# Planned durations of a list scheduler taken anew from a trace, in an attention kernel followed by two feed-forward blocks

## The chip, the cores and the metric

The kernel runs on one core of one Trainium2 chip, in one launch. The metric is device time in microseconds (us). Five engines work side by side: TensorE (PE, with its weight loads PEld), VectorE (DVE), ScalarE (ACT), GpSimd (POOL) and SyncE (SP, which issues the transfers). Each takes its instructions strictly in the order in which they were written.

## The reference

```
scores = q @ k.T / sqrt(64)              # 4 batches, 8 heads, 576 x 64, float32
kth    = the 32nd largest score of each row
attn   = softmax of the scores >= kth, 0 elsewhere
x      = (attn @ v), heads side by side   # 2304 tokens x 512
h      = x @ w_in;  g = max(0.01*h, h);  x = g @ w_out        # 512 -> 2048 -> 512
h      = max(x @ w1, x @ w2, x @ w3);    out = h @ w_out2     # 512 -> 768 -> 512
```

The weights are float64. The outputs are float32.

## The kernel before

**Work.** Attention is cut into 72 steps, numbered here 0 to 71, 18 to a batch; so steps 18, 36 and 54 open a new batch. A step takes 128 query rows of two heads, or 64 rows of four. Its parts are: the score product on PE (L702, two halves, j = 0 and j = 1), a copy of each half out of PSUM by ACT (L707, into one of three buffers S), the search for the 32nd largest score on DVE (L722 MAX8 and L724 MATCH_REPLACE8, seven rounds for each half), the exponential on ACT (L772), the mask (L777 on DVE for one half; L781 on DVE and L784 on POOL for the other), a split of the result in two float16 halves (L786 on ACT, L788 on POOL), a transposing transfer, the product with v on PE (L816 to L818) and its scaling (L823 and L825 on DVE, L827 on ACT).

The tokens that come out are grouped in 10 units (u = 0 to 9) of 192, 128, six times 256, 192 and 256 tokens. Each unit runs through both feed-forward blocks, on PE three float16 matmuls (L859 to L861) for each product: h (`h<-xu,wi`), y (`acc<-f16t,wo`), the three products m of the second block (`h<-k,w`, with a maximum on DVE, L1000), and o (`acc<-f16t,w`). Of float64 weights, DVE makes float32 by shifts on their two halves (L484, L487, L490: 42 pieces, so 126 instructions), ACT and POOL scale and split them (L352 to L354).

**What sets the order.** `Plan` is a list scheduler that runs when the kernel is built. Each piece of work is handed to `op(engine, duration, function, ...)` with a planned duration, what it reads and writes, and a due time `pr` (a step is due 11.9 us after the one before, `TA`). `Plan.run` then plays the engines forward with these durations: on each engine, of the pieces that could start at the earliest time (within `eps`, 0.03 us), the one with the lowest due time goes next, and a buffer is taken when the plan says that it is free. The planned start times give the order in which the instructions are written. The durations are not otherwise used: on the chip each engine runs its stream in that order and waits where data is late.

Durations come from small formulas:

```
def mm(n):                    return (n / 2.4 + MMO) / 1000
def act(n, psum=False, aps=0): return (n * 0.833 + (70 if psum else 120) + 105 * aps) / 1000
def dve(n, fast=False):       return (n / (2 if fast else 1) / 0.96 + 69) / 1000
def pool(n):                  return (n * 2.13 + 110) / 1000
```

The line numbers below are those of the kernel before; in the changed kernel every number from L49 on is higher by 3 (L722 is L725 there).

Of the kernel before, what the change touches and what calls it, by code (L numbers as in the profile page):

```python
# [14 lines left out]
AF = mybir.ActivationFunctionType  # L15
# [3 lines left out]
B, H, S, D = 4, 8, 576, 64  # L19
# [23 lines left out]


EPS = 0.03
MMO = 3.0
PQ = 100.0
PA = 100.0
PB = 0.0  # L49
# [22 lines left out]
class Plan:  # L72
# [50 lines left out]
    def run(self):  # L123
# [10 lines left out]
        while len(order) < total:  # L134
# [45 lines left out]
                    slots[b.tag].sort()  # L180
            for m in n.succ:
                m.nd -= 1
                m.ready = max(m.ready, end + self.LAT.get((n.eng, m.eng), 0.2))
                if m.nd == 0:
                    pend[m.eng].append(m)
        order.sort()
# [33 lines left out]
def attention_moe_kernel(ctx, tc, qk, v, w_in, w_out, w123, w2o, outT):  # L220
# [242 lines left out]
    def prep_w(kind, c, parts, hi, lo, colnorm, n2c, s, bi, pr, tags, guard=((), (), []), gate=()):  # L463
# [8 lines left out]
        for i, saps in enumerate(parts):  # L472
            nf = sum(n for _, n in saps)
            f = buf(tags[1], [P, 768 if tags[1] == "raw" else 512], I32)
            o = 0
            for sap, n in saps:
                raw = buf(tags[0], [P, 768])
                op(SP, 0.55, lambda raw=raw, sap=sap, n=n: Y.dma_start(raw().bitcast(I64)[:, :n], sap),
                   w=[raw, (key, "ld")] + ([(f, "ld")] if tags[1] in ("raw", "k2") or tags[0] == "raw" else []),
                   r=list(gate) + zr + (zf + [("l1", hp, a) for hp in range(HP) for a in range(2)] * (kind == "z") + guard[2] * (tags[1] == "raw") if kind in "tz" else []), pr=PRW0 if (kind, c) == ("i", 0) else pr,  # L480
                   dma=dma(P * n * 8))
                w = lambda raw=raw, n=n: raw().bitcast(I32)[:, :2 * n].rearrange("p (n t) -> p n t", t=2)
                t = lambda f=f, n=n, o=o: f()[:, o:o + n]
                op(DVE, dve(n, True), lambda w=w, t=t: V.tensor_scalar(  # L484
                    t(), w()[:, :, 1], 3, 0x3FFFFFFF, op0=ALU.logical_shift_left, op1=ALU.bitwise_and),
                   r=[raw] + zr + zf, w=[(f, o)], pr=pr)
                op(DVE, dve(n), lambda w=w, t=t: V.scalar_tensor_tensor(  # L487
                    t(), w()[:, :, 0], 29, t(), op0=ALU.logical_shift_right, op1=ALU.bitwise_or),
                   r=[raw] + zr + zf, w=[(f, o)], pr=pr)
                op(DVE, dve(n), lambda w=w, t=t: V.scalar_tensor_tensor(  # L490
                    t(), w()[:, :, 1], -0x40000000, t(), op0=ALU.bitwise_and, op1=ALU.bitwise_or),
                   r=[raw] + zr + zf, w=[(f, o)], pr=pr)
                for q in range(0, n, 512):
                    m = min(n - q, 512)
                    sq.append(((f, o), lambda f=f, q=q + o, m=m: f()[:, q:q + m].bitcast(F32), m))
                o += n
            fs.append((f, [(f, x) for x in np.cumsum([0] + [n for _, n in saps[:-1]]).tolist()],
                       lambda f=f, n=nf: f()[:, :n].bitcast(F32), nf))
# [181 lines left out]
    def attention(i):  # L680
# [10 lines left out]
        for j in range(2):  # L691
# [10 lines left out]
                            T.matmul(p()[osl, h, o:o + w], q()[:, hh, st, :n], k()[:, hh, kc:kc + w],  # L702
                                     start=st == 0, stop=st == 1, skip_group_check=True)

            op(PE, (0.5 if full else 0.7) * (COLD if i < NCOLD else 1), qk_, r=[k] + [(q, x) for x in range(3)], w=[p], pr=pq)
            t = Sb[j]
            op(ACT, act(S, True), lambda t=t, p=p: A.activation(t().rearrange("p (a s) -> p a s", a=2),  # L707
                                                               p()[:, :, :288], AF.Copy), r=[p], w=[(Sp, j)], pr=pq)
# [2 lines left out]
        if md == "N":  # L711
# [3 lines left out]
            for g in range(7):  # L715
                for j in range(2):
                    r = g // 2
                    mc = lambda j=j, r=r: m()[:, j, 8 * r:8 * r + 8]
                    src = (lambda j=j: Sb[j]()) if g < 2 else (lambda j=j: wj(j))
                    rd = [(Sp, j)] if g < 2 else [(wp, j, 0)]  # L720
                    if g % 2 == 0:
                        op(DVE, dve(S) * 1.03, lambda mc=mc, src=src: V.max(mc(), src()), r=rd, w=[(m, j, 0, r)], pr=pd)  # L722
                    else:
                        op(DVE, dve(S) * 1.03 + 0.06, lambda mc=mc, src=src, j=j: V.match_replace(  # L724
                            out=wj(j), in_to_replace=mc(), in_values=src(), imm_value=NEG),  # L725
                           r=[(m, j, 0, r)] + rd, w=[(wp, j, 0)], pr=pd)
        else:
# [73 lines left out]
        for j in range(2):  # L801
# [15 lines left out]
                        T.matmul(o[:, 0:64], hc, vl, start=False, stop=False, skip_group_check=True)  # L817
                        T.matmul(o, lc, vh, start=False, stop=c == 4, skip_group_check=True)  # L818

            op(PE, 15 * mm(64) * (1 if full else 2) * (COLD if i < NCOLD else 1), avm, r=[pt] + [(vt, x) for x in range(3)], w=[avb, (xs, "a"), (xhl, "a", i)], pr=pa)  # L820
        nh = 2 if full else 4
        r = buf("r", [P, 8])
        op(DVE, 0.07, lambda: V.tensor_scalar(r()[:n, 0:nh], av()[:n, 0:nh, 64:65].rearrange("p h e -> p (h e)"),  # L823
# [54 lines left out]
    def ffn(u, pr0, between=None):  # L878
# [14 lines left out]
        def h_tile(f):  # L893
# [4 lines left out]
            for k in range(KC):  # L898
# [1 line left out]
                                             lambda x: xu()[:, x, k, :N], k == 0, k == KC - 1),  # L900
                   r=xk + wk, w=[p], pr=pr)
            rr = fbuf("k2", "H", [P, 2, UN])
            op(ACT, act(N, True, 1), lambda: A.activation(rr()[:, 0, :N], p()[:, :N], AF.Prelu,  # L903
                                                          scale=SC["e"][:, c:c + 1], alpha=0.01),
               r=[p, "e_in"], w=[(rr, 0)], pr=pr)
            gs[f] = hilo(rr, pr, "H")

        def hilo(g, pr, ph):
            hl = fbuf("f16t", ph, [P, 2, UN], F16)
            op(ACT, act(N), lambda: A.activation(hl()[:, 0, :N], g()[:, 0, :N], AF.Copy), r=[(g, 0)], w=[(hl, 0)],  # L910
               pr=pr)
            if u >= (DL if ph == "H" else DM_):
                op(DVE, dve(N), lambda: V.tensor_tensor(hl()[:, 1, :N], g()[:, 0, :N], hl()[:, 0, :N],
# [259 lines left out]
```

## Time and profile before

| | us |
|---|---|
| median of 3 runs (1161.68 to 1165.74) | 1161.78 |
| time of the profiled execution | 1165.0 |
| its span, from the first to the last instruction | 1163.2 |
| DVE busy | 998.8 (86%) |
| PE busy | 923.0 (79%) |
| ACT busy | 758.5 (65%) |
| POOL busy | 728.9 (63%) |

Busy times of one engine are a union of its instructions' spans; where two instructions overlap by a few tens of ns, that time counts once. The table of stages below cuts the span at the places of which the prediction speaks.

### The profile page before, as it was taken

The page shows a single profiled execution, that of the slowest core. Times are in us where ns is not written, and L with a number is a line of the kernel's source. Part 1 is how long each engine was busy: PE and PEld are TensorE (multiplying, and loading weights), DVE is VectorE, ACT ScalarE, POOL GpSimd, SP SyncE. Part 2 cuts the span into 40 slices and gives each one's busy share as a digit, 9 for nine tenths or more (in the row PEclk, how much of TensorE's full clock was granted, in tenths as well). Part 3 has the DMA queues.
Part 4 walks back from the last instruction along what each step waited for, and adds up shares of the span by engine and source line. Part 5 has one row for each costly group of instructions (what it writes and reads, how often), then busy time and mean ns, then how long its engine had stood idle before and what let it go on. Part 6 is the DMA issues. An engine that isn't in the chain of part 4 may idle for free.

```text
span 1163.2 us, 27290 instructions
## 1 busy us (share of the span) xinstructions
PE 923.0 (79%) x10294; PEld 807.4 (69%) x10294; DVE 998.8 (86%) x2106; ACT 758.5 (65%) x1625; POOL 728.9 (63%) x1054
## 2 busy tenths in 40 slices
PE   3252234675389899789899978998999999999998
PEld 2131223664289788678788867887988898898987
DVE  3999999999999999899996999989989999994001
ACT  7666566777567766547777865677787667564341
POOL 5577885797546766547777664567787557464231
PEclk9965555796589999899999999999999999999999
DMA  7756518554563543334466433554473332332000
GB/s 229 250 150 219 181 25 234 158 140 113 123 148 66 103 81 69 63 71 117 95 163 160 86 73 61 101 128 107 98 177 87 82 82 55 69 69 56 15 1 19
DMA packets 268548, 125.78 MB, mean 108 GB/s; under 512 B 237440, under 2 KB 255360, under 8 KB 266368
## 3 DMA queue, kind: packets, MB, share of 16 engines
q1 hardware_dynamic: 268416, 124.04, 43.4%
q8 instruction: 81, 1.33, 0.5%
q14 instruction: 51, 0.42, 0.1%
HBM read 62.65 MB, written 14.16 MB: 66 GB/s over the span
## 4 chain that ended last, share of the span: by engine, by line
PE 51%; DVE 20%; POOL 8%; ACT 7%; DMA 7%; issue 4%; SPq 1%; POOLq 0%; ACTq 0%; DVEq 0%
PE h L859 9%; PE h L860 9%; PE h L861 9%; DMA pt<-phl 6%; PE acc L860 5%; PE acc L861 5%; PE acc L859 5%; DVE m L722 5%; DVE w L724 4%; PE s L702 3%; DVE w L487 3%; DVE w L490 2%; POOL phl L788 2%; PE av L816 2%; DVE w L484 2%
## 5 line engine op out<-in xcount | busy, mean ns | idle before, releaser
L722 DVE MAX8 m<-w 128x8 f32<-128x576 f32 x432 | 310.2, 747 | 0.3
L916 POOL TENSOR_TENSOR f16t<-k,f16t 128x256 f16<-128x256 f32 (+2 forms) x220 | 143.4, 654 | 183.6 <-ACT f16t L910 174.9
L788 POOL TENSOR_TENSOR phl<-pp,phl 128x576 f16<-128x576 f32 x144 | 189.8, 1325 | 36.3 <-ACT phl L786 35.2
L724 DVE MATCH_REPLACE8 w<-m,w 128x576 f32<-128x576 f32 x288 | 212.1, 741 | 0.0
L859 PE MATMUL h<-k,w 128*128 128x256 f16 (+2 forms) x720 | 189.9, 268 | 22.1 <-ACT k L956 8.3
L860 PE MATMUL h<-k,w 128*128 128x256 f16 (+2 forms) x720 | 190.0, 268 | 5.2 <-POOL k L958 4.8
L861 PE MATMUL h<-k,w 128*128 128x256 f16 (+2 forms) x720 | 190.1, 268 | 0.0
L860 PE MATMUL acc<-f16t,wo 128*128 128x256 f16 (+2 forms) x640 | 167.3, 265 | 7.7 <-POOL f16t L916 7.7
L859 PE MATMUL acc<-f16t,wo 128*128 128x256 f16 (+2 forms) x640 | 167.4, 265 | 0.7 <-ACT f16t L910 0.7
L861 PE MATMUL acc<-f16t,wo 128*128 128x256 f16 (+2 forms) x640 | 167.3, 265 | 0.0
L859 PE MATMUL h<-xu,wi 128*128 128x256 f16 (+1 forms) x576 | 156.2, 271 | 4.4 <-ACT k L903 3.7
L702 PE MATMUL s<-kt,qt 128*128 128x288 f16 (+5 forms) x800 | 109.6, 287 | 60.0 <-ACT S L707 45.2
L860 PE MATMUL h<-xu,wi 128*128 128x256 f16 (+1 forms) x576 | 156.3, 271 | 0.0
L861 PE MATMUL h<-xu,wi 128*128 128x256 f16 (+1 forms) x576 | 156.2, 271 | 0.0
L786 ACT ACTIVATE phl<-pp 128x576 f16<-128x576 f32 x144 | 97.0, 681 | 63.4 <-DVE pp L777 24.0
L772 ACT ACTIVATE pp<-S,nb,colt 128x576 f32<-128x576 f32 x144 | 121.7, 860 | 16.3 <-POOL nb L762 11.3
L784 POOL TENSOR_TENSOR pp<-pp,S 128x576 f32<-128x576 f32 x72 | 93.7, 1301 | 58.3 <-DVE S L781 34.8
L910 ACT ACTIVATE f16t<-k 128x256 f16<-128x256 f32 (+2 forms) x220 | 85.7, 392 | 58.5 <-DVE k L1000 55.8
L860 PEld LDWEIGHTS <-w 128*128 128x128 f16 x960 | 95.3, 99 | 36.8 <-issue 27.9
L702 PEld LDWEIGHTS <-qt 128*128 128x128 f16 (+1 forms) x800 | 64.5, 109 | 79.4 <-issue 54.9
L903 ACT ACTIVATE k<-h,colt 128x256 f32<-128x256 f32 (+2 forms) x160 | 71.3, 449 | 69.9 <-PE h L861 67.8
L707 ACT ACTIVATE S<-s 128x576 f32<-128x576 f32 x144 | 92.7, 644 | 36.0 <-PE s L702 30.0
(136 smaller groups left out, 2709.4 us busy)
## 6 DMA issues: line engine op xcount, KB each, us to landing
w<-in_w SPq DMA_DIRECT2D x18, 512.0 KB, 4.4
w<-in_w_in SPq DMA_DIRECT2D x8, 1024.0 KB, 7.5
w<-in_w_out SPq DMA_DIRECT2D x8, 1024.0 KB, 4.9
raw<-in_qk SPq DMA_DIRECT2D x24, 288.0 KB, 3.3
dqk<-hl SPq DMA_DIRECT2D x48, 144.0 KB, 2.5
kt<-dqk SPq DMA_DIRECT2D x16, 288.0 KB, 3.2
qt<-dqk SPq DMA_DIRECT2D x144, 32.0 KB, 2.3
raw<-in_v SPq DMA_DIRECT2D x12, 352.0 KB, 3.6
```

Source lines behind the costliest of these rows:

```text
L702: T.matmul(p()[osl, h, o:o + w], q()[:, hh, st, :n], k()[:, hh, kc:kc + w], start=st == 0, stop=st == 1, skip_group_check=True)
L707: op(ACT, act(S, True), lambda t=t, p=p: A.activation(t().rearrange("p (a s) -> p a s", a=2), p()[:, :, :288], AF.Copy), r=[p], w=[(Sp, j) ...
L722: op(DVE, dve(S) * 1.03, lambda mc=mc, src=src: V.max(mc(), src()), r=rd, w=[(m, j, 0, r)], pr=pd)
L724: op(DVE, dve(S) * 1.03 + 0.06, lambda mc=mc, src=src, j=j: V.match_replace(out=wj(j), in_to_replace=mc(), in_values=src(), imm_value=NEG) ...
L772: op(ACT, act(S, aps=2), lambda j=j, es=es: A.activation(pp()[:, j], Sb[j](), AF.Exp, bias=nb()[:, j:j + 1], scale=es[:, 0:1]), r=[(Sp, j) ...
L784: op(POOL, pool(S), lambda j=j: G.tensor_tensor(p2(j), p2(j), mk(j), op=ALU.mult), r=[(Sp, j)], w=[(pp, j)], pr=pr)
L786: op(ACT, act(S), lambda j=j: A.activation(phl()[:, 0, j], pp()[:, j], AF.Copy), r=[(pp, j)], w=[(phl, 0, j)], pr=pr)
L788: op(POOL, pool(S), lambda j=j: G.tensor_tensor(phl()[:, 1, j], pp()[:, j], phl()[:, 0, j], op=ALU.subtract), r=[(pp, j), (phl, 0, j)], w= ...
L859: T.matmul(out, wt(0), xt(0), start=first, stop=False, skip_group_check=True)
L860: T.matmul(out, wt(0), xt(1), start=False, stop=False, skip_group_check=True)
L861: T.matmul(out, wt(1), xt(0), start=False, stop=last, skip_group_check=True)
L916: op(POOL, pool(N) + 0.044, lambda: G.tensor_tensor(hl()[:, 1, :N], g()[:, 0, :N], hl()[:, 0, :N], op=ALU.subtract), r=[(g, 0), (hl, 0)], ...
```

## The change

No instruction is added, removed or altered. Planned durations get other values: a matmul 1 ns more; the three weight conversions on DVE 1.5 and 1.35 times as long; a score product 0.54 for 0.5 us; MAX8 0.672 us for 0.689 and MATCH_REPLACE8 0.690 for 0.749; the product with v by 66 columns for 64; of ACT's instructions between two feed-forward products, L903 0.055 and L910 0.035 us more. `LX`, a further delay between engines, is put in with the value 0.

```diff
-MMO = 3.0
+MMO = 4.0
+LX = 0.0
+WC1 = 1.5
+WC2 = 1.35
...
-                m.ready = max(m.ready, end + self.LAT.get((n.eng, m.eng), 0.2))
+                m.ready = max(m.ready, end + self.LAT.get((n.eng, m.eng), 0.2) + LX * (n.eng != m.eng))
...
-                op(DVE, dve(n, True), lambda w=w, t=t: V.tensor_scalar(
+                op(DVE, dve(n, True) * WC1, lambda w=w, t=t: V.tensor_scalar(
...
-                op(DVE, dve(n), lambda w=w, t=t: V.scalar_tensor_tensor(
+                op(DVE, dve(n) * WC2, lambda w=w, t=t: V.scalar_tensor_tensor(
...
-            op(PE, (0.5 if full else 0.7) * (COLD if i < NCOLD else 1), qk_, ...
+            op(PE, (0.54 if full else 0.75) * (COLD if i < NCOLD else 1), qk_, ...
...
-                        op(DVE, dve(S) * 1.03, lambda mc=mc, src=src: V.max(mc(), src()), ...
+                        op(DVE, 0.672, lambda mc=mc, src=src: V.max(mc(), src()), ...
...
-                        op(DVE, dve(S) * 1.03 + 0.06, lambda mc=mc, src=src, j=j: V.match_replace(
+                        op(DVE, 0.69, lambda mc=mc, src=src, j=j: V.match_replace(
...
-            op(PE, 15 * mm(64) * (1 if full else 2) * (COLD if i < NCOLD else 1), avm, ...
+            op(PE, 15 * mm(66) * (1 if full else 2) * (COLD if i < NCOLD else 1), avm, ...
...
-            op(ACT, act(N, True, 1), lambda: A.activation(rr()[:, 0, :N], p()[:, :N], AF.Prelu,
+            op(ACT, act(N, True, 1) + 0.055, lambda: A.activation(rr()[:, 0, :N], p()[:, :N], AF.Prelu,
...
-            op(ACT, act(N), lambda: A.activation(hl()[:, 0, :N], g()[:, 0, :N], AF.Copy), ...
+            op(ACT, act(N) + 0.035, lambda: A.activation(hl()[:, 0, :N], g()[:, 0, :N], AF.Copy), ...
```

The order that comes out differs on every engine. Three places show it.

PE, behind the last product with v (the last two rows of it, then what follows): `w` with 192 columns is the second block of unit 8, `wo` with 192 columns the second product of its first block. Before:

```order
L818 LDWEIGHTS pt_16111
L818 MATMUL av_16174<-vt_12597,pt_16111 64x65
L859 LDWEIGHTS w_76
L859 MATMUL h_16237<-k_2120_15907,w_76 128x192
L860 LDWEIGHTS w_76
L860 MATMUL h_16237<-k_2121_15911,w_76 128x192
```

and in the changed kernel:

```order
L821 LDWEIGHTS pt_15913
L821 MATMUL av_15975<-vt_12005,pt_15913 64x65
L862 LDWEIGHTS wo
L862 MATMUL acc_15361<-f16t_15963,wo 128x192
L863 LDWEIGHTS wo
L863 MATMUL acc_15361<-f16t_15963,wo 128x192
```

The last product with v has moved ahead in the stream: behind it stand 672 feed-forward matmuls of 256 columns in both orders, and of 192 columns 156 before and 300 now.

PE, the first half of step 55's score product, the second step of the last batch (`h<-k,w` is the second block of unit 5, `acc<-f16t,wo` the first block of unit 6). Before:

```order
L860 MATMUL acc_12061<-f16t_12112,wo 128x256
L861 LDWEIGHTS wo
L861 MATMUL acc_12061<-f16t_12112,wo 128x256
L702 LDWEIGHTS qt_12109
L702 MATMUL s_12172<-kt_11351,qt_12109 128x288
```

and now:

```order
L863 MATMUL h_11628<-k_1557_11338,w_76 128x256
L864 LDWEIGHTS w_76
L864 MATMUL h_11628<-k_1556_11333,w_76 128x256
L705 LDWEIGHTS qt_11560
L705 MATMUL s_11634<-kt_11465,qt_11560 128x288
```

It stands earlier in the feed-forward work, and the work that stood ahead of it now stands ahead of step 56. Between the second half of one step's score product and that of the next stand, from step 54 to 55, 55 to 56 and 56 to 57, 243, 105 and 96 feed-forward matmuls of 256 columns before (444), and 60, 330 and 111 now (501). At the batch switch before, from step 35 to step 38, it is 477 before and 501 now.

DVE, where the search of step 8 begins (its first MAX8 reads S_1362), among weight conversions of 512 columns. Before:

```order
L484 TENSOR_SCALAR w_76<-w_77 128x512
L825 RECIPROCAL r_1668<-r_1668 128x2
L722 MAX m_1679<-S_1362 128x8
L487 SCALAR_TENSOR_TENSOR w_76<-w_77,w_76 128x512
L326 TENSOR_SCALAR colt<-h_1672 128x1
```

and now:

```order
L490 SCALAR_TENSOR_TENSOR w_76<-w_77,w_76 128x512
L725 MAX m_1846<-S_1362 128x8
L493 SCALAR_TENSOR_TENSOR w_76<-w_77,w_76 128x512
L487 TENSOR_SCALAR k_311_1763<-w_77 128x512
L725 MAX m_1846<-S_1362 128x8
```

The conversions stand further ahead: 64 of the 126 stood before this place, and 83 do now (38 and 48 ahead of step 5, 80 and 99 ahead of step 9; 126 ahead of step 14 in both).

## Rows read from the trace of the kernel before

**Rows 1.** The page: busy time by engine, and DVE in 40 slices.
```profile
PE 923.0 (79%) x10294; PEld 807.4 (69%) x10294; DVE 998.8 (86%) x2106; ACT 758.5 (65%) x1625; POOL 728.9 (63%) x1054
DVE  3999999999999999899996999989989999994001
```

**Rows 2.** Busy time by stage (the first row names the columns).
```profile
core 0: us, PE busy (x) PEld busy (x) DVE busy (x) ACT busy (x) POOL busy (x), PEclk, DMA share, GB/s
0.00:40.00 40.00, 13.76 (x54) 8.50 (x54) 19.92 (x43) 30.21 (x56) 23.30 (x75) 1.00 0.78 243
40.00:323.00 283.00, 124.42 (x1246) 100.88 (x1247) 276.95 (x502) 183.81 (x339) 206.46 (x227) 0.65 0.55 154
323.00:619.00 296.00, 269.62 (x3299) 238.35 (x3299) 276.55 (x620) 202.84 (x462) 186.10 (x301) 0.95 0.46 100
619.00:833.00 214.00, 196.98 (x2194) 172.24 (x2192) 201.25 (x449) 150.40 (x333) 136.71 (x195) 1.00 0.44 97
833.00:871.00 38.00, 37.47 (x388) 33.08 (x386) 33.42 (x72) 31.85 (x71) 32.91 (x53) 1.00 0.70 168
871.00:1055.00 184.00, 178.50 (x2081) 160.99 (x2078) 178.52 (x392) 124.03 (x283) 114.81 (x156) 0.99 0.33 76
1055.00:1069.50 14.50, 14.50 (x211) 14.18 (x209) 3.04 (x10) 4.48 (x13) 7.21 (x12) 0.91 0.18 42
1069.50:1159.10 89.60, 87.72 (x836) 79.20 (x835) 9.11 (x23) 29.91 (x73) 21.46 (x38) 1.00 0.03 7
```

**Rows 3.** The same view, two stretches of feed-forward work alone, 192 and 256 columns.
```profile
1070.00:1082.00 12.00, 12.00 (x146) 12.00 (x145) 2.51 (x6) 4.29 (x13) 2.30 (x4) 1.00 0.08 13
1090.00:1120.00 30.00, 30.00 (x278) 26.89 (x276) 0.00 (x0) 10.39 (x24) 7.77 (x12) 1.00 0.01 1
```

**Rows 4.** What DVE waited for, 323 to 1056 us (total, times, longest).
```profile
DVE r L823 <- PE av L818: 15.0, 24, 1.4
DVE k L1000 <- PE h L861: 9.0, 13, 2.9
DVE m L722 <- ACT S L707: 8.4, 5, 3.5
DVE colt L326 <- PE acc L965: 4.6, 5, 1.5
DVE colt L326 <- PE h L312: 1.8, 5, 0.6
```

**Rows 5.** DVE's timeline at two batch switches: the second halves of step 37, then step 56.
```profile
629.10 0.76 DVE L722 MAX8 m<-S 128x8 f32<-128x576 f32 x1 [3.54 <-ACT S L707]
...
858.50 0.76 DVE L722 MAX8 m<-S 128x8 f32<-128x576 f32 x1 [2.88 <-ACT S L707]
```

**Rows 6.** Conversions of 1024 columns, 0 to 323 us (count | busy, mean ns).
```profile
L484 DVE TENSOR_SCALAR w<-w 128x1024 int32<-128x1024 int32 x16 | 17.7, 1106 | 1.3 <-DMA w<-in_w_in 1.3
L490 DVE SCALAR_TENSOR_TENSOR w<-w 128x1024 int32<-128x1024 int32 x9 | 17.5, 1950 | 0.0
L487 DVE SCALAR_TENSOR_TENSOR w<-w 128x1024 int32<-128x1024 int32 x9 | 13.6, 1512 | 0.0
```

**Rows 7.** Single conversions in DVE's timeline (start, duration).
```profile
11.30 1.23 DVE L490 SCALAR_TENSOR_TENSOR w<-w 128x1024 int32<-128x1024 int32 x1
...
137.83 2.48 DVE L484 TENSOR_SCALAR w<-w 128x1024 int32<-128x1024 int32 x1
...
140.35 3.03 DVE L487 SCALAR_TENSOR_TENSOR w<-w 128x1024 int32<-128x1024 int32 x1
...
146.19 0.68 DVE L484 TENSOR_SCALAR w<-w 128x1024 int32<-128x1024 int32 x1
...
146.90 1.23 DVE L487 SCALAR_TENSOR_TENSOR w<-w 128x1024 int32<-128x1024 int32 x1
```

**Rows 8.** POOL's timeline beside them.
```profile
136.65 5.64 POOL L354 TENSOR_TENSOR wo<-w,wo 128x1024 f16<-128x1024 f32 x2
142.27 1.16 POOL L333 TENSOR_SCALAR colt<-colt 128x1 int32<-128x1 int32 x1
```

More of the change, by code (lines that the diff above doesn't have):

```diff
@@ L483, in prep_w @@
                 t = lambda f=f, n=n, o=o: f()[:, o:o + n]
-                op(DVE, dve(n, True), lambda w=w, t=t: V.tensor_scalar(
+                op(DVE, dve(n, True) * WC1, lambda w=w, t=t: V.tensor_scalar(
                     t(), w()[:, :, 1], 3, 0x3FFFFFFF, op0=ALU.logical_shift_left, op1=ALU.bitwise_and),
                    r=[raw] + zr + zf, w=[(f, o)], pr=pr)
-                op(DVE, dve(n), lambda w=w, t=t: V.scalar_tensor_tensor(
+                op(DVE, dve(n) * WC2, lambda w=w, t=t: V.scalar_tensor_tensor(
                     t(), w()[:, :, 0], 29, t(), op0=ALU.logical_shift_right, op1=ALU.bitwise_or),
                    r=[raw] + zr + zf, w=[(f, o)], pr=pr)
-                op(DVE, dve(n), lambda w=w, t=t: V.scalar_tensor_tensor(
+                op(DVE, dve(n) * WC2, lambda w=w, t=t: V.scalar_tensor_tensor(
                     t(), w()[:, :, 1], -0x40000000, t(), op0=ALU.bitwise_and, op1=ALU.bitwise_or),
@@ L703, in qk_ @@
                                      start=st == 0, stop=st == 1, skip_group_check=True)
-            op(PE, (0.5 if full else 0.7) * (COLD if i < NCOLD else 1), qk_, r=[k] + [(q, x) for x in range(3)], w=[p], pr=pq)
+            op(PE, (0.54 if full else 0.75) * (COLD if i < NCOLD else 1), qk_, r=[k] + [(q, x) for x in range(3)], w=[p], pr=pq)
             t = Sb[j]
@@ L721, in attention @@
                     if g % 2 == 0:
-                        op(DVE, dve(S) * 1.03, lambda mc=mc, src=src: V.max(mc(), src()), r=rd, w=[(m, j, 0, r)], pr=pd)
+                        op(DVE, 0.672, lambda mc=mc, src=src: V.max(mc(), src()), r=rd, w=[(m, j, 0, r)], pr=pd)
                     else:
-                        op(DVE, dve(S) * 1.03 + 0.06, lambda mc=mc, src=src, j=j: V.match_replace(
+                        op(DVE, 0.69, lambda mc=mc, src=src, j=j: V.match_replace(
                             out=wj(j), in_to_replace=mc(), in_values=src(), imm_value=NEG),
@@ L818, in avm @@
                         T.matmul(o, lc, vh, start=False, stop=c == 4, skip_group_check=True)
-            op(PE, 15 * mm(64) * (1 if full else 2) * (COLD if i < NCOLD else 1), avm, r=[pt] + [(vt, x) for x in range(3)], w=[avb, (xs, "a"), (xhl, "a", i)], pr=pa)
+            op(PE, 15 * mm(66) * (1 if full else 2) * (COLD if i < NCOLD else 1), avm, r=[pt] + [(vt, x) for x in range(3)], w=[avb, (xs, "a"), (xhl, "a", i)], pr=pa)
         nh = 2 if full else 4
@@ L909, in hilo @@
             hl = fbuf("f16t", ph, [P, 2, UN], F16)
-            op(ACT, act(N), lambda: A.activation(hl()[:, 0, :N], g()[:, 0, :N], AF.Copy), r=[(g, 0)], w=[(hl, 0)],
+            op(ACT, act(N) + 0.035, lambda: A.activation(hl()[:, 0, :N], g()[:, 0, :N], AF.Copy), r=[(g, 0)], w=[(hl, 0)],
                pr=pr)
```

## The prediction

> **What bounds the kernel now.** Four views were read: the page for the engines' shares, the table by stage for where each engine is full, DVE's waits and its timeline for what holds it up, and the written order of both kernels for what stands behind what.
>
> The page shows DVE busy 86% of the span and at nine tenths or more in almost every slice until the last three, where it does next to nothing [rows 1]. The table cuts this into stages [rows 2]. From 40 to 1055 us DVE is busy 277.0 of 283, 276.6 of 296, 201.3 of 214, 33.4 of 38 and 178.5 of 184 us: 48 us idle in 1015. The searches of the 72 steps pace everything here. At 1055 us the last mask of step 71 is done. In the next 14.5 us that step's result passes ACT, POOL and the transposing transfer, and PE ends the last product with v at 1069.5 us. Then PE alone is full, 87.7 of 89.6 us until its last matmul ends at 1159.1, and 4.1 us of closing work remain to the end of the span, 1163.2.
>
> So the time is a sum: DVE's time to the last mask (its work, which the change leaves as it is, and its idle time), 14.5 us for the last step to reach PE, what stands on PE behind the last product with v, and 4.1 us. The profiled execution took 1165.0 us, 3.2 over the median of the three runs, 1161.8. The sum is made against 1165.0 and 3.2 is taken off at the end. One measurement of this kernel can tell about 0.5%, 5.8 us, from no change.
>
> **Part 1: the tail on PE grows, +11.8 us.** Behind the last product with v stood 672 feed-forward matmuls of 256 columns and 156 of 192; now it is 672 and 300 (the first piece of order above). A matmul of 256 columns takes 30.00 us / 278 = 108 ns there, one of 192 columns 12.00 / 146 = 82.2 ns [rows 3]. Check on the tail before: 672 x 0.108 + 156 x 0.0822 = 85.4 us of the 89.6. The new 144 cost 144 x 0.0822 = 11.8 us. Nothing hides them: once the last product is done, no other work is left, and PE was full already. The planner now takes a search for shorter and a matmul for longer, so it lets attention run ahead of the feed-forward work. That work is the same, so it is left over at the end. The gain to set against it must come from DVE's idle time before 1055 us.
>
> **Part 2: the batch switches hold DVE longer, +9.6 us.** When a batch begins, the plan puts a lump of feed-forward matmuls between two score products. DVE works off the copies S that it has, and then waits: 3.54 us before the second half of step 37 and 2.88 us before step 56 [rows 5], together the greater part of its 8.4 us of waits for S [rows 4]. PE was busy 37.5 of 38 us at the second place [rows 2], so each matmul that is added there moves the next S back. From step 54 to step 57 the matmuls rise from 444 to 501: 57 x 0.108 = 6.2 us, and two more halves of the product with v stand there too (30 matmuls of 65 columns; at most as long as the 82.2 ns of one of 192, 2.5 us; I take 0.8). At the switch before, 477 become 501: 24 x 0.108 = 2.6 us. DVE had no S in reserve at either place, so I take the whole, 7.0 + 2.6 = 9.6 us. The bounds are 0, if PE comes to each lump earlier by as much because it has less to do before, and 9.6.
>
> **Part 3: DVE waits less for PE elsewhere, -15.2 us.** Between 323 and 1056 us DVE waited for PE's products at L823, L1000 and L326: 15.0 + 9.0 + 4.6 + 1.8 = 30.4 us, 47 times, none longer than 2.9 us [rows 4]. These are instructions that the plan wrote into the search at a time at which PE was not yet there. With PE planned slower and the search faster, PE is ahead of its place in the plan, and such waits shrink. The bounds are 0 and -30.4. L823 is the largest, and it waits for the end of a long row (ACT, POOL, transfer, PE) of which only PE's part is planned otherwise. So I take half, -15.2 us.
>
> **Part 4: the conversions come earlier, 0.** Ahead of step 8's search stand 83 conversions in place of 64, and all 126 are done by step 14 in both. DVE is full from 40 to 323 us (277.0 of 283), so the exchange of two pieces of its work moves nothing by itself, and the feed-forward work that starts sooner finds PE with room (124.4 of 283 busy) [rows 2]. What could move is how long a conversion takes. One of 1024 columns takes 1.11 us (L484), 1.51 (L487) and 1.95 (L490) in the mean [rows 6], and 0.68, 1.23 and 1.23 where it runs alone [rows 7]. Over these 34 instructions the excess is 16 x 0.43 + 9 x 0.28 + 9 x 0.72 = 15.9 us, 0.47 each. I take it as unchanged. The bounds are -15.9, if all of it went, and the same upward.
>
> The rows show what the excess is. L484 at 137.83 us took 2.48 us and ended at 140.31, and the L487 behind it 3.03, to 143.38 [rows 7]. POOL ran two splits of weights from 136.65 to 142.29, of 2.82 us each, so their ends are 139.47 and 142.29 [rows 8]. Each conversion ends 0.84 and 1.09 us behind the end of a split, about its time alone. It stood still until POOL was through.
>
> The Trainium skill says why (SBUF — State Buffer, "Who interferes with whom"): DVE, in a two-port mode or with two inputs in SBUF, and GpSimd share a port pair under an exclusive lock, and the later one blocks until the first is done. These rows agree with it. By that rule no factor of 1.5 or 1.35 belongs to a conversion at all: in a new order its price depends on POOL's neighbours there, and a factor from one trace need not hold in the next. That is the second rival below; by the factors the sum keeps its 0 here.
>
> **Sum.** +11.8 + 9.6 - 15.2 + 0 = +6.2 us. 1165.0 + 6.2 = 1171.2 in the profiled execution, 1168.0 against the median: slower by 0.5%, on the edge of what can be measured. The parts are opposed, so the sign hangs on part 3.
>
> **The rivals.**
>
> *DVE's waits go altogether (faster).* If the plan's times are now true enough that PE is never late outside the lumps, part 3 is -30.4; and if PE, with less ahead of it, comes to each lump early, part 2 is 0. The sum is then 11.8 - 30.4 = -18.6 us, 1143; halfway to it from my forecast is 1155.6. It decides where parts 2 and 3 together fall below -17.6 us, for then the sum passes -5.8. For it: PE was 178.5 of 184 us busy from 871 to 1055 [rows 2], so it had little room, and the work taken out of that stage gives it some. Against: in that same stage DVE was idle for 5.5 us alone, and not even all of that can go. 0.18.
>
> *Conversions meet POOL more often (clearly slower).* Nineteen more conversions are packed ahead of step 8, beside splits of which each holds POOL for 2.8 us. If each of them costs the mean excess once more, 19 x 0.47 = 8.9 us, the sum is 15.1 and the time 1176.9; if each stood still as the one at 137.83 (2.48 - 0.68 = 1.80 us), it would be 34.2 us, the far end. For it: such meetings are in the rows. Against: the number of splits is the same, and those that conversions meet early they don't meet later. 0.20.
>
> *Only the order moves (no change).* The reserve of S takes up part 2, part 3 is a little more than 11.8, and the time stays within 5.8 us of 1161.8. For it: DVE has the same work, and was busy for 967 of 1015 us. Against: the tail's 144 matmuls are sure. 0.22.
>
> My forecast, the sum with its terms near the values taken, gets 0.40.
>
> **How the numbers follow.** The forecast spreads from 1162 to 1176, as part 3 is 5 us less or more and part 2 between 5 and 9.6; a little over half of it, 0.25, lies above 1167.6, the rest within 0.5%. Slower: 0.25 + 0.20 and a little of the third, 0.47. Same: 0.15 + 0.18 = 0.33. Faster: 0.20, the first rival and the low edge of the third. The range reaches down to 1150, half of the first rival and more, and up to 1186, the second rival at twice its small price. Its likeliest case is 1168.
>
> **What the profile of the changed kernel will show.** Part 1: PE works for about 101 us behind the last product with v, with some 980 matmuls in place of 836; if it is under 95, part 1 is wrong. Part 2: DVE's waits for S (now at L725) rise from 8.4 to some 18 us, the longest ahead of step 56 or 57. Part 3: DVE's waits at L826, L1003 and L329 in the middle fall from 30 to 15 us. Part 4: step 14's search begins near 323 us, as before; if it begins 5 us sooner or later, the conversions moved the time, and the busy time of L487, L490 and L493 will tell. The forecast is wrong if the last mask is done before 1043 us (a gain that pays for the tail) or after 1062.

## The result, and the profile after

The changed kernel takes 1179.45 us (median of 4 runs, 1177.0 to 1181.99) against 1162.64 (4 runs, 1161.68 to 1165.74): ratio 1.0140, 95% interval 1.0109 to 1.0171. The change makes the kernel slower by 1.4%. The forecast was 1168, slower by 0.5%, in a range of 1150 to 1186. The profiled execution took 1181.99 us, 17.0 more than the one before.

The page after, the two lines that answer to [rows 1]:

```profile
PE 920.8 (78%) x10294; PEld 804.4 (68%) x10294; DVE 990.8 (84%) x2106; ACT 762.6 (65%) x1625; POOL 717.2 (61%) x1054
DVE  2999999989999999999967999999859999991001
```

DVE is busy for 8.0 us less than before, in a span that is 17.0 longer. The dips of its slices at the two batch switches are deeper: a 6 and a 7 around 620 us, where one slice had a 6, and an 8 and a 5 around 855, where one had an 8.

To see where the time went, both traces were cut at the same pieces of work: at the start of the search of steps 14, 36, 38, 54 and 57 (found by their place in the written order), at the end of the last mask, and at the end of the last product with v. The table of stages of the kernel before, with these cuts (columns as in [rows 2], here and below; the stages behind the last mask are the last two there):

```profile
40.00:323.20 283.20, 124.42 (x1246) 100.88 (x1247) 277.15 (x504) 184.01 (x339) 206.66 (x227) 0.65 0.55 154
323.20:599.30 276.10, 249.93 (x3032) 220.77 (x3032) 261.47 (x584) 189.71 (x435) 171.07 (x260) 0.95 0.45 96
599.30:637.60 38.30, 37.85 (x482) 33.44 (x480) 27.62 (x64) 27.48 (x60) 29.50 (x59) 1.00 0.63 162
637.60:832.70 195.10, 178.52 (x1980) 156.09 (x1978) 188.21 (x422) 135.55 (x300) 121.77 (x176) 1.00 0.43 90
832.70:870.60 37.90, 37.37 (x387) 33.00 (x385) 33.36 (x73) 31.75 (x71) 32.78 (x55) 1.00 0.71 170
870.60:1055.00 184.40, 178.90 (x2085) 161.34 (x2082) 178.88 (x392) 124.44 (x283) 115.21 (x156) 0.99 0.33 76
```

The same view of the changed kernel:

```profile
40.00:327.20 287.20, 124.61 (x1255) 100.50 (x1254) 274.75 (x506) 187.06 (x343) 202.77 (x230) 0.66 0.53 152
327.20:589.90 262.70, 235.42 (x2949) 210.70 (x2948) 255.02 (x577) 182.08 (x415) 164.00 (x250) 0.98 0.47 94
589.90:638.60 48.70, 45.03 (x546) 38.92 (x544) 29.57 (x70) 35.48 (x77) 34.71 (x67) 1.00 0.67 155
638.60:825.50 186.90, 168.97 (x1847) 146.69 (x1844) 185.83 (x415) 130.94 (x288) 114.95 (x168) 0.98 0.42 96
825.50:879.30 53.80, 49.12 (x515) 43.41 (x513) 37.17 (x83) 38.04 (x83) 38.17 (x63) 0.99 0.56 121
879.30:1060.90 181.60, 172.90 (x1967) 153.36 (x1965) 177.31 (x390) 117.93 (x263) 106.12 (x146) 0.99 0.38 73
...
1072.00:1176.10 104.10, 100.17 (x982) 91.26 (x982) 11.77 (x30) 35.34 (x89) 26.39 (x50) 1.00 0.04 6
```

A stage's length less DVE's busy time is DVE's idle time. Worked out so from these rows:

| stage | length before, after | DVE idle before, after |
|---|---|---|
| 40 us to step 14 | 283.2, 287.2 | 6.0, 12.4 |
| step 14 to 36 | 276.1, 262.7 | 14.6, 7.7 |
| 36 to 38 (batch switch) | 38.3, 48.7 | 10.7, 19.1 |
| 38 to 54 | 195.1, 186.9 | 6.9, 1.1 |
| 54 to 57 (batch switch) | 37.9, 53.8 | 4.5, 16.6 |
| 57 to the last mask | 184.4, 181.6 | 5.5, 4.3 |
| last mask to last product with v | 14.5, 11.1 | |
| behind it, to PE's last matmul | 89.6, 104.1 | |

Up to the last mask DVE's idle time rises by 12.9 us and its work falls by 7.0 (966.7 to 959.7), so the mask is 5.9 later. The step to PE is 3.4 shorter, the tail 14.5 longer: 5.9 - 3.4 + 14.5 = 17.0, the whole difference. Each ordinary stage behind step 14 has become quicker, and each batch switch slower by more than had been won up to it (10.4 us against the 9.4 won up to step 36, then 15.9 against the 8.2 won from 38 to 54). In the two switches PE was busy for 45.0 of 48.7 us and 49.1 of 53.8, before for 37.9 of 38.3 and 37.4 of 37.9. So more of PE's work fell into them, 7.2 and 11.8 us, and PE itself now stood idle in them, for 3.7 and 4.7 us.

What DVE waits for between step 14 and the last mask, to be held against [rows 4]:

```profile
DVE m L725 <- ACT S L710: 14.9, 5, 6.7
DVE r L826 <- PE av L821: 12.3, 16, 2.7
DVE colt L329 <- PE h L315: 11.0, 4, 6.0
DVE k L1003 <- PE h L864: 5.8, 7, 1.9
```

Waits for S went from 8.4 to 14.9 us, and one that had been next to nothing (1.8 us) is 11.0: L329 for a total that PE takes at L315. DVE's timeline shows where, at the first switch (first row) and at the second:

```profile
631.98 0.76 DVE L725 MAX8 m<-S 128x8 f32<-128x576 f32 x1 [6.66 <-ACT S L710]
...
851.99 0.16 DVE L329 TENSOR_SCALAR colt<-h 128x1 int32<-128x1 int32 x1 [3.55 <-PE h L315]
...
860.30 0.16 DVE L329 TENSOR_SCALAR colt<-h 128x1 int32<-128x1 int32 x1 [6.02 <-PE h L315]
...
879.32 0.76 DVE L725 MAX8 m<-S 128x8 f32<-128x576 f32 x1 [4.11 <-ACT S L710]
```

The waits at 851.99 and 860.30 belong to the preparation of the next batch's q and k, the scale that a split needs. The other engines at 860 show what it was waiting for itself, the load of the raw values:

```profile
859.88 0.38 PE L315 MATMUL h<-colt,ones 128*128 128x1 f32 x2 [1.36 <-ACT junk L344]
...
859.05 0.68 ACT L344 ACTIVATE junk<-raw 128x576 bf16<-128x576 f32 x1 [0.52 <-DMA raw<-in_qk]
```

Load, squares on ACT, total on PE, power of two on DVE, split, transfer, score product: this row of work for the new batch is late, the plan fills PE with feed-forward matmuls meanwhile, and DVE, which has come early, stands.

Why the load is late can be read from SyncE, which issues the transfers in order (its waits at L1041 from 826 to 862 us: in total, times, longest; then two pieces of its timeline):

```profile
SPq L1041 <- ACT k L1031: 8.7, 3, 8.1
...
839.04 6.94 SPq L1041 DMA_DIRECT2D out_T<-k  x12
...
847.40 0.59 SPq L373 DMA_DIRECT2D raw<-in_qk  x1
```

Its queue stood for 8.1 us at the stores of a finished piece of output, for which ACT (L1031) was not yet there. The load of raw values (L373) came behind those stores, at 847.40 us, and the next one at 855.04; the profile names no wait of these loads themselves. No run moved the stores, so that they make the row late is read and not tested.

### The profile page after: what moved, and what is told of

Same layout as the page of the kernel before. It is cut to its first block, busy times and chain, and to the rows that moved or that the text cites. A ratio compares the mean times of both kernels' runs of the same rounds, so it can differ in the third digit from the quotient of the medians.

```text
span 1180.2 us, 27312 instructions
## 1 busy us (share of the span) xinstructions
PE 920.8 (78%) x10294; PEld 804.4 (68%) x10294; DVE 990.8 (84%) x2106; ACT 762.6 (65%) x1625; POOL 717.2 (61%) x1054
## 4 chain that ended last, share of the span: by engine, by line
DVE 39%; PE 25%; DMA 10%; POOL 9%; issue 7%; ACT 7%; SPq 1%; POOLq 0%; ACTq 0%; DVEq 0%
DVE m L725 14%; DVE w L727 13%; DMA pt<-phl 7%; PE h L862 4%; PE h L863 4%; PE h L864 4%; PE acc L863 2%; PE acc L862 2%; PE acc L864 2%; DVE S L784 2%; DVE k L1003 2%; POOL phl L791 2%; DVE w L490 2%; DVE w L493 2%; DVE pp L780 2%
## 5 line engine op out<-in xcount | busy, mean ns | idle before, releaser
L789 ACT ACTIVATE phl<-pp 128x576 f16<-128x576 f32 x144 | 97.5, 680 | 94.9 <-DVE pp L780 44.0
L819 PE MATMUL av<-vt,pt 128*128 128x65 f16 (+1 forms) x800 | 92.3, 203 | 42.1 <-DMA pt<-phl 31.3
L705 PEld LDWEIGHTS <-qt 128*128 128x128 f16 (+1 forms) x800 | 64.4, 107 | 79.4 <-issue 53.8
L725 DVE MAX8 m<-S 128x8 f32<-128x576 f32 x144 | 104.2, 745 | 16.4 <-ACT S L710 16.4
```

The costliest lines, as they stand in the source:

```text
L725: op(DVE, 0.672, lambda mc=mc, src=src: V.max(mc(), src()), r=rd, w=[(m, j, 0, r)], pr=pd)
L789: op(ACT, act(S), lambda j=j: A.activation(phl()[:, 0, j], pp()[:, j], AF.Copy), r=[(pp, j)], w=[(phl, 0, j)], pr=pr)
L819: T.matmul(o, hc, vh, start=c == 0, stop=False, skip_group_check=True)
```

## The experiments

All times are medians, all ratios are to runs of the kernel before on the same chip, with their 95% intervals. "Step 14 begins", "36 to 38" and the like are read with the cuts above, from one profiled execution of each kernel; so a small difference of one stage has no interval.

### The search's prices alone (e1)

The kernel before with MAX8 and MATCH_REPLACE8 at the new prices:

```diff
-op(DVE, dve(S) * 1.03, lambda mc=mc, src=src: V.max(...
+op(DVE, 0.672, lambda mc=mc, src=src: V.max(...
-op(DVE, dve(S) * 1.03 + 0.06, lambda mc=mc, ...: V.match_replace(...
+op(DVE, 0.69, lambda mc=mc, ...: V.match_replace(...
```

> The kernel before with the two search prices of the change alone (MAX8 0.672, MATCH_REPLACE8 0.690); all other planned durations as before. By the written order its tail behind the last product with v is 300 matmuls of 192 columns, as in the changed kernel, and the lump of feed-forward work at the last batch switch stands ahead of step 56 as there (from step 53 to 57 64.7 us of matmuls at 0.109 us, changed kernel 64.4, before 54.9). Theory (the search prices make the tail and the lump, and these make the loss): slower than before by 10 to 18 us, 1172 to 1181. Rival A (the early conversions or the matmul prices make it): within 5 us of before, 1158 to 1168.

Measured: 1176.39 us, ratio 1.0101 (1.0068 to 1.0134). The table of stages at the early part, the two switches and the tail (in this order):

```profile
40.00:316.40 276.40, 119.56 (x1214) 95.52 (x1214) 274.59 (x495) 181.60 (x334) 197.48 (x225) 0.83 0.56 154
582.50:629.30 46.80, 46.21 (x526) 39.51 (x526) 27.65 (x63) 35.00 (x75) 33.92 (x70) 0.96 0.64 160
821.80:873.40 51.60, 48.79 (x508) 43.28 (x507) 35.41 (x83) 35.47 (x80) 34.98 (x60) 1.00 0.58 131
1065.30:1169.50 104.20, 100.29 (x983) 91.32 (x982) 11.77 (x30) 35.46 (x89) 26.42 (x50) 1.00 0.03 6
```

The tail (104.2 us, 983 matmuls) and both switches (46.8 and 51.6 us) are those of the changed kernel, from these two prices alone. Step 14 begins 6.8 us earlier than before (2.6 of it is work of DVE, four conversions among it, that now stands behind that place) and step 36 16.8 earlier, but step 57 2.8 later: what was won is lost in the two switches. Not all of it goes at the first: step 38 still begins 8.3 us earlier. The last mask ends 1.0 us earlier than before, so what makes this run slower is the tail, 14.6 us longer. The search's prices make the change's gain and most of its loss.

### All prices but the search's (e2)

The changed kernel with the search's prices of before (the diff above, turned round).

> The changed kernel with the two search prices set back. By the written order its tail is that of before (156 matmuls of 192 columns) and the lump stands ahead of step 55 as before (60.2 us from step 53 to 57). Theory: most of the loss goes; +4 us from the early stage as in the changed kernel and some 3 from a lump a little longer than before, so 1162 to 1171. Rival A: 1174 or more.

Measured: 1192.31 us, 1.0240 (1.0216 to 1.0265), slower than the changed kernel by about a per cent. My theory missed this: it had the conversions at nothing. The tail is that of before (89.6 us), yet step 8 begins 41.8 us late and step 14 16.8 late, and DVE is idle for 23.9 us from 40 us to there, 6.0 before. Its two largest waits in that stretch:

```profile
DVE colt L519 <- PE h L514: 10.4, 5, 7.3
DVE r L826 <- PE av L821: 6.1, 6, 2.0
```

L519 takes the maximum over PE's sums of squared weight columns; before (L516) it waited 0.8 us in that stretch. The timeline around the longest such wait, from four engines (start, duration, idle time before it):

```profile
124.27 1.21 DVE L490 SCALAR_TENSOR_TENSOR w<-w,w 128x1024 int32<-128x1024 int32 x1
125.40 0.68 DVE L487 TENSOR_SCALAR w<-w 128x1024 int32<-128x1024 int32 x1
126.00 1.21 DVE L493 SCALAR_TENSOR_TENSOR w<-w,w 128x1024 int32<-128x1024 int32 x1
...
127.27 1.21 DVE L490 SCALAR_TENSOR_TENSOR w<-w,w 128x1024 int32<-128x1024 int32 x1
128.51 1.23 DVE L493 SCALAR_TENSOR_TENSOR w<-w,w 128x1024 int32<-128x1024 int32 x1
137.06 0.23 DVE L519 TENSOR_REDUCE colt<-h 128x1 f32<-128x64 f32 x1 [7.32 <-PE h L514]
...
124.41 2.96 POOL L594 TENSOR_SCALAR colt<-colt 128x8 f32<-128x8 f32 x1
127.32 1.21 POOL L613 TENSOR_TENSOR colt<-colt 128x1 f32<-128x1 f32 x1
132.04 0.19 POOL L336 TENSOR_SCALAR colt<-colt 128x1 int32<-128x1 int32 x1
...
132.27 1.15 ACT L355 ACTIVATE w<-w,colt 128x1024 f32<-128x1024 f32 x1 [5.90 <-POOL colt L336]
134.41 0.61 ACT L508 ACTIVATE junk<-w 128x512 bf16<-128x512 f32 x1
135.07 0.59 PE L514 MATMUL h<-junk,ones 128*128 128x64 bf16 x8 [8.07 <-ACT junk L508]
```

Read it from the end. DVE waited for PE, PE for ACT's squares (L508), which stood behind L355, which had waited 5.90 us for a scale that POOL computes (L336). POOL was late in part because tiny instructions ahead of it were long beside DVE's packed conversions: L594, L613 and L615 took 2.96, 1.21 and 1.24 us, in the changed kernel 0.28, 0.20 and 0.27. That is 4.7 us more, against ACT's wait of 5.90. DVE's lead ran round through three engines and came back as a wait of its own. This accounts for the longest wait, 7.32 of the 23.9 us, and not for all: over the whole stretch POOL's 74 one-column scale instructions (L336 and L338) took 27.4 us here and 31.5 before (L333 and L335).

### The conversions' prices alone (e5)

The kernel before with `WC1 = 1.5` and `WC2 = 1.35` alone:

```diff
-op(DVE, dve(n, True), lambda w=w, t=t: V.tensor_scalar(
+op(DVE, dve(n, True) * WC1, lambda w=w, t=t: V.tensor_scalar(
...
-op(DVE, dve(n), lambda w=w, t=t: V.scalar_tensor_tensor(
+op(DVE, dve(n) * WC2, lambda w=w, t=t: V.scalar_tensor_tensor(
```

> The kernel before with the two new factors for the weight conversions alone (1.5 and 1.35). Theory: these two prices make the early loss of e2. With them 97 conversions stand ahead of step 8's search (64 before), and DVE comes to the maxima over squared weight columns, which PE still has to sum, too soon. So DVE stands idle for 15 to 30 us between 40 us and step 14's search (6.0 before, 14.4 in the changed kernel, 23.9 in e2), that search begins 8 to 22 us later than before, and with a tail of some 7 us more the time is 1168 to 1192. Rival: the loss comes from the prices of PE and ACT (matmul, score product, product with v, L906, L913). Then step 14's search begins within 4 us of before, and the time is 1155 to 1168.

Measured: 1186.30 us, 1.0178 (1.0147 to 1.0208), the largest effect of any group of prices. The early stage:

```profile
40.00:333.90 293.90, 127.83 (x1278) 104.19 (x1279) 280.20 (x505) 189.25 (x347) 200.37 (x231) 0.83 0.53 149
```

Step 14 begins 10.7 us late, in the theory's range and outside the rival's. DVE's idle time, 13.7 us from 40 us on, is a little below the 15 expected; 6.2 us of it are waits of L519 and 4.7 of L826. (The changed kernel's 14.4 in the expectation is 12.4 by the table above.) The tail grew by 7.9 us, to 97.5.

### All prices but the conversions' (e6)

The changed kernel with `WC1 = WC2 = 1.0`.

> The changed kernel with the two conversion factors back at 1.0. Theory (conversion prices make the early loss): DVE is idle for less than 6 us between 40 us and step 14's search, and this search begins 3 to 12 us earlier than in the kernel before; behind the last product with v PE still works for 100 to 106 us, since the search's and the matmuls' prices stay. Time 1160 to 1174. Rival (prices of PE and ACT): step 14's search begins 2 to 8 us later than in the kernel before, as in the changed kernel, and the time is 1174 to 1186.

Measured: 1175.46 us, 1.0090 (1.0059 to 1.0121).

```profile
40.00:319.10 279.10, 116.88 (x1223) 93.74 (x1224) 279.08 (x494) 182.12 (x335) 199.49 (x224) 0.68 0.55 152
```

DVE is busy for 279.08 of 279.10 us: the early waits are gone with the factors, and step 14 begins 4.1 us before that of the kernel before. So the factors made the early loss, as the theory said; the total is 1.5 us above its range. The last mask ends 1.2 us earlier than before, since the switches took the lead back again (the first is 51.4 us long), and the tail is 107.0 us, 17.4 more than before.

### PE's and ACT's prices alone (e11)

The kernel before with `MMO = 4.0`, score product 0.54, product with v by 66 columns, and the additions of 0.055 and 0.035 us (as in the diff of the change).

> The kernel before with the new prices of PE and ACT alone (a matmul 1 ns more, score product 0.54, product with v by 66 columns, L906 0.055 and L913 0.035 us more). By the order nothing more is left behind the last product with v (86.0 us of matmuls as before, counted as in e9), and the lumps are 50.4 and 60.2 (52.0 and 54.9 before). Theory: these prices alone change little: step 14 begins within 5 us of before, the tail is 88 to 92 us, the time 1160 to 1172. Rival: they slow the middle (in e2 and e6 step 38 to 46 took 10 and 7 us longer), the last mask is over 10 us later than before and the time over 1174.

Measured: 1166.65 us, 1.0008 (0.9987 to 1.0028). Step 14 begins 3.6 us earlier, the last mask ends 1.5 later, the tail is 89.5 us. The theory held. The three groups alone come to 1.0, 1.8 and 0.1%, together to 1.4: they don't add up. The conversions' factors pull 97 conversions ahead of step 8 by themselves, and only 83 beside the new search prices.

### The next batch's preparation due earlier (e3 and e4)

`LB` sets how many us ahead of its first step a batch's preparation is due, for the third and fourth batch. In the changed kernel:

```diff
-    LB = 60
+    LB = 100
```

> The changed kernel with the preparation of q and k of batches 2 and 3 due 40 us earlier in the plan (LB 60 to 100), nothing else. By the written order the lumps at both batch switches are gone (from step 35 to 38 20.3 us of feed-forward matmuls in place of 54.6, from step 53 to 57 36.0 for 64.4); the tail grows from 97.8 to 111.0 us. In the changed kernel the switches cost DVE 21 us at steps 36 to 38 (48.7 us for two steps of which DVE's work is some 28) and 22 us at 54 to 57 (53.8 for some 32). Theory (PE's lumps stop the search): the last mask comes some 40 us earlier, the tail 13 later: 1179 - 27 = 1152, 1146 to 1160. Rival B (the lumps lie where q and k are late anyway, so taking them away gains nothing): 1175 to 1195, with the tail's 13 us on top.

Measured: 1165.63 us, 1.0008 (0.9984 to 1.0033).

```profile
595.40:620.60 25.20, 25.20 (x317) 22.52 (x315) 25.20 (x58) 19.62 (x41) 19.81 (x36) 1.00 0.60 138
1043.80:1159.70 115.90, 113.42 (x1145) 104.64 (x1144) 11.77 (x30) 39.72 (x102) 30.27 (x57) 1.00 0.02 6
```

The switches fall from 48.7 and 53.8 us to 25.2 and 35.5 (54 to 57), DVE is never idle in the first, and the last mask ends 30.7 us earlier than in the changed kernel. So the late preparation and the lumps that come with it are what holds DVE at the switches. The lever moves both at once, so this run doesn't say how much each costs. Of the 41.8 us won at the two switches 11.1 are lost again in the other stages, the step from the last mask to PE is 2.5 us longer and the tail 11.8 longer: 16.4 us reach the profiled execution's time. I had expected 1146 to 1160. The tail's 13 us were counted; that the other stages would take part of the gain was not.

The kernel before with `LB = 140`:

> The kernel before with the preparation of q and k of batches 2 and 3 due 80 us earlier (LB 60 to 140), nothing else. The lumps are gone (27.1 us for 52.0 from step 35 to 38, 42.2 for 54.9 from 53 to 57), the tail is 80.4 us of matmuls for 86.0. The switches cost DVE 12 and 6 us before. Theory: 18 us less at the switches and 5.6 in the tail: 1162 - 24 = 1138, 1134 to 1148. Rival B: 1156 to 1168.

Measured: 1151.76 us, 0.9897 (0.9864 to 0.9930), faster than both kernels, between theory and rival.

```profile
1065.80:1149.70 83.90, 81.98 (x767) 73.50 (x767) 8.27 (x21) 28.74 (x70) 20.95 (x37) 1.00 0.03 8
```

From 36 to 38 it takes 23.0 us, 15.3 less, yet the last mask ends only 1.1 us earlier, since step 36 begins 7.4 us late (the preparation is now done ahead of it) and the rest is lost in ordinary stages. Of the 9.4 us that the profiled execution gains, 5.7 are the tail, 2.6 the step from the last mask to PE, and 1.1 the mask. By the medians the gain is 12.7 us.

### The preparation due later (e9)

The kernel before with `LB = 40`, the same lever in the other direction.

> The kernel before with LB 40 for 60: the next batch's preparation is due later still. By the order the lump from step 35 to 38 grows from 52.0 to 92.2 us of matmuls (counted at 0.327 us for three of 256 columns), the one from 53 to 57 stays (54.6, 54.9 before), and 3.2 us less is left behind the last product with v. Theory (a lump is paid for by DVE): step 36 to 38 takes 70 to 80 us (38.3 before), the last mask is 22 to 40 us later than before and the time 1178 to 1200. Rival (PE's sum decides, since it is 91 to 98% busy from 323 us on): what PE does in the lump is missing behind it, DVE runs there with fewer waits, the last mask is at most 15 us later, and the time is 1158 to 1176.

Measured: 1213.02 us, 1.0414 (1.0385 to 1.0442), even above the theory's range.

```profile
596.90:680.10 83.20, 82.53 (x887) 72.62 (x888) 28.47 (x65) 47.15 (x105) 46.12 (x91) 1.00 0.37 89
```

PE works through the lump, 82.5 of 83.2 us, and DVE for 28.5: 54.7 us idle, 44.0 more than before. Of the 54.7, 21.5 are waits for the preparation's totals (L326) and 10.0 for S. Nothing of it comes back, and the last mask ends 52.2 us late. DVE has as much to do behind the lump as before, and PE's head start doesn't shorten that. The rival is out. Here too the lump and the late preparation move together.

### Three attempts at a better order (e7, e8, e10)

The new search prices with `LB = 200`; the old prices with `LB = 180`; the old prices with 90 for the third batch and 160 for the fourth (`else LB` becomes `else 90 if b == 2 else 160`).

> The kernel before with the two new search prices and the next batch's preparation due 200 us ahead (LB 200 for 60). In the order, 235 and 354 matmuls of 256 columns stand in the two lumps (477 and 444 before), and as many behind the last product with v as before. Theory: the three terms add up. Step 14 begins 5 to 10 us earlier (as in e1), step 36 to 38 takes 22 to 27 us, 54 to 57 35 to 39, the tail is 84 to 92 us: 1138 to 1150. Rival: PE is so full behind step 36 that what is won ahead of it and at the lumps comes back as waits elsewhere, so the last mask is no earlier than in e4 (1053.9): 1150 to 1160.

> The kernel before with LB 180 for 60 (e4 had 140). The lumps are as in e4 by the order (27.5 and 39.6 us of matmuls, counted), but 3.7 us less of matmuls are left behind the last product with v. Theory: a tail that is shorter by 3.7 us is won outright: tail 79 to 82 us, last mask as in e4 (1053.9 give or take 3), time 1144 to 1151. Rival: work that isn't left for the end delays DVE ahead of it by as much: last mask 1056 to 1060, time 1151 to 1157.

> The kernel before, with the preparation of the third batch due 90 us ahead and of the fourth 160 (60 before; e4 140 for both, e8 180 for both). Counted as in e9, 19.3 us of matmuls stand in the first lump and 40.5 in the second, 76.7 behind the last product with v. Theory: third-batch preparation that comes less early than in e4 and e8 leaves DVE alone in steps 18 to 36 (step 36 at most 6 us later than before), the tail is 79 to 82 us as in e8, and the time is 1140 to 1150. Rival: DVE waits elsewhere for PE by as much, so the time is 1150 to 1158.

Measured: 1164.29 us, 1.0001 (0.9982 to 1.0020); 1155.17, 0.9921 (0.9893 to 0.9948); 1153.24, 0.9904 (0.9882 to 0.9927). The stage from step 14 to 36 of the three:

```profile
316.40:611.00 294.60, 266.35 (x3277) 238.48 (x3278) 263.74 (x602) 204.36 (x462) 178.20 (x283) 0.94 0.46 105
```
```profile
322.60:613.40 290.80, 265.58 (x3251) 237.51 (x3251) 264.77 (x596) 201.43 (x461) 182.36 (x288) 0.95 0.48 103
```
```profile
321.80:607.60 285.80, 259.98 (x3165) 230.80 (x3164) 264.87 (x593) 199.75 (x454) 178.46 (x279) 0.97 0.49 105
```

Each has its switch from 36 to 38 at 22.8 to 23.5 us and its tail where the order put it (88.1, 81.3 and 81.3 us), as foretold. But this stage is 18.5, 14.7 and 9.7 us longer than before's 276.1, with DVE idle for 30.9, 26.0 and 20.9 of it (14.6 before): with preparation due earlier, DVE waits more there, mostly for products with v and of the feed-forward blocks (L823 13.4 and L1000 10.0 us in e8, 5.9 and 4.4 before) and, in e7 and e10, for the exponential (9.1 and 4.9). Why these come late was not followed further. So the theory of e7 missed by 14 us (and its rival by 4), that of e8 by 4 and that of e10 by 3; the last two ended in their rivals' ranges. In e8 it is the time alone that did: the last mask, at 1054.9 us, is where the theory had it. In e10 step 36 begins 8.3 us late, outside the 6 allowed, and in e7 the last mask, at 1055.6, is no earlier than e4's, as its rival said. By their intervals e8 and e10 can't be told from e4, which stays the fastest order found: 1.0% below the kernel before, and 2.4% below the changed one (0.9897 / 1.0140 = 0.976).

## Why the prediction was right and where it was not

The time lay in the range and on the right side. That says little of the terms: the range was 36 us wide, and the profiled execution became slower by 17.0 us where the sum had 6.2. The median also lies 2.6 us from the price of the second rival, 1176.9, whose mechanism didn't come; so the hit owes something to luck. The terms came out so.

**Part 1, the tail: right.** Said were 11.8 us, 101 us of PE's work and some 980 matmuls; 982 are there, with 100.17 us of work, 12.5 more than before. Another 2.0 us is PE's idle time in the tail (1.9 to 3.9), which I had not foreseen. It comes from the search's prices: alone they make the same tail, and PE's and ACT's prices make none. The conversions' prices alone make 7.9 us of tail, which do not add to it. Of my two reasons, a shorter search and a longer matmul, the first was enough.

**Part 2, the batch switches: right place, size far off.** Said were 9.6 us; DVE's idle time rose by 8.4 and 12.1, 20.5 together. The step that failed is "the bounds are 0 ... and 9.6". I added up the matmuls that came to stand in the lump and held DVE's arrival fixed. But the lump ends with the row of preparation and PE's work, by their clock: DVE came 9.4 us earlier to step 36, and step 38 began 1.0 us later than before; it came 7.2 us earlier to step 54, and step 57 began 8.7 us later. Read as delays of the switches' ends, the lumps' prices (2.6, and 9.6 with the second) came near; it was the gain in front of them that could not be kept. What part 3 won was waited away here. I also looked for waits for S alone. They rose to 14.9 us, not to some 18, and the longest, 6.66 us, came in step 37 and not ahead of step 56 or 57; over half of the second switch's 16.6 us was L329 waiting for a total of that preparation (3.55 and 6.02 us).

**Part 3, DVE's waits elsewhere: right size, wrong meaning.** DVE's idle time in the three ordinary stages behind step 14 fell from 27.0 to 13.0 us, by 14.0; I had said 15.2. By line the foretold fall from 30.4 to 15 us did not come (L826, L1003 and L329 are 29.1 together by the rows shown), since L329's new waits at the switches count among them. The forecast treated parts 2 and 3 as independent terms, and they are not: a gain ahead of a switch is worth only what the switch lets through (nothing in the changed kernel; in e1 8.3 of 16.8 us at the first switch).

**Part 4, the conversions: wrong in both halves, partly cancelling.** Said was 0, with bounds of 15.9 either way from their duration. They got shorter: up to step 14 the three lines took 130.5 us, 135.8 before, worked out from their busy time. But DVE stood idle for 6.4 us more, and step 14 began 4.0 us late. The step that failed is "DVE is full from 40 to 323 us (277.0 of 283), so the exchange of two pieces of its work moves nothing by itself". Full was the old order's property. With the conversions' prices alone (e5), DVE comes to L519 and L826 before PE has what they ask for; without them (e6) it is not idle at all. In the changed kernel itself the 6.4 us are spread: L519 waits 2.7 us in this stage (0.8 before), L826 3.3 (2.1), and conversions for their loads or a buffer 3.7 (2.0).

The changed kernel's rows for [rows 6] show the three lines:

```profile
L487 DVE TENSOR_SCALAR w<-w 128x1024 int32<-128x1024 int32 x16 | 18.9, 1188 | 1.6 <-DMA w<-in_w_in 1.6
L493 DVE SCALAR_TENSOR_TENSOR w<-w 128x1024 int32<-128x1024 int32 x9 | 15.7, 1741 | 0.0
L490 DVE SCALAR_TENSOR_TENSOR w<-w 128x1024 int32<-128x1024 int32 x9 | 13.4, 1489 | 0.0
```

In the order of these rows the means were 1106, 1950 and 1512 ns: a plan that lengthened all three met one that grew and two that shrank.

**The rivals.** "DVE's waits go altogether" is out: parts 2 and 3 came to +6.5, not -17.6. "Conversions meet POOL more often" is out as it was priced: DVE's conversions did not get longer: up to step 14 they took 130.5 us in the changed kernel and 131.9 in e2, 135.8 before. (e1's 133.8 are those of 122 conversions; four come later there.) In one place of e2 it was POOL that paid, 2.96 us for 0.28, which went round to DVE as a wait. "Only the order moves" is out by the interval.

**The sum.** In the terms of the table, +6.4 early, +20.5 at the switches, -14.0 elsewhere, -7.0 of DVE's work, -3.4 to the last product (why was not looked into), +14.5 of tail. The forecast's terms with the same meaning were 0, +9.6, -15.2, 0, 0 and +11.8.

What stays open: that DVE waits at the switches for the next batch's preparation and the lump was tested by moving the preparation's due time, which moves both. Which piece of that row ends last (the loads' buffers, SyncE's queue, the totals on PE) was not tried by itself; the trace points to SyncE's queue at the second switch. That conversions stretch POOL's small instructions is read from one trace beside another; no run took the conversions away from beside them.

## What to carry to other kernels

A plan with durations taken anew from a trace is not by that a better plan. Its due times and lead times (here `LB`) stayed as they were, and one lead time by itself was worth more, 1.0% faster, than all the durations. When a forecast adds a gain on a waiting engine to a later stall of the same engine, ask first by whose clock the stall ends; if it is another engine's, the gain in front of it can be lost in part or whole. And judge an order where work is left over, as well as where a wait goes: in most runs here a stage that got shorter came back in part as a longer one, or as a longer tail.

## What the runs showed of the hardware

Tiny instructions on POOL are not always cheap beside a full DVE. In e2 L594 (128x8) took 2.96 us and L613 (128x1) 1.21 while conversions of 1024 columns ran one behind the other on DVE, and 0.28 and 0.20 in the changed kernel:

```profile
124.10 0.28 POOL L594 TENSOR_SCALAR colt<-colt 128x8 f32<-128x8 f32 x1
124.33 0.20 POOL L613 TENSOR_TENSOR colt<-colt 128x1 f32<-128x1 f32 x1
```

The Trainium skill (SBUF — State Buffer, "Who interferes with whom") has DVE and GpSimd under one exclusive lock, with the later one blocked until the first is done. L613 agrees: it began 0.05 us behind a conversion and ended 0.05 us behind its end (127.27 to 128.48). L594 shows more: it began 0.14 us behind a conversion (124.27) and ended 0.16 us behind the end of the third in a row (126.00 to 127.21), so it did not come in between conversions that followed each other closely. Both show the side that I had left out: the one blocked may be POOL, and with it whoever waits for POOL.

PE's granted clock is a mean over its two levels of 1.2 and 2.4 GHz. In the stage from 40 us to step 14, in which PE is under half busy, it was 0.65 in the profiled execution of the kernel before and 0.83 in those of e1 and e5. That need not come from the prices: in four executions of e1 alone the mean over the span was 0.898 to 0.942. Nor does the time follow it. The stage took 276.4 us in e1 and 293.9 in e5 at the same 0.83; and of 39 executions of the kernel before, 26 with a mean of 0.895 to 0.916 took 1165.0 us on average, 13 with 0.933 to 0.957 took 1165.3.
